# Order of the row minima over PSUM banks, what an exp waits for, and the planned price of a division

## The chip, the cores and the metric

One core of a Trainium2 chip runs one launch. The metric is the device time of the launch in microseconds. Five queues work side by side on the core: PE (TensorE, matrix products), DVE (VectorE), ACT (ScalarE), POOL (GpSimd) and SP (SyncE, which issues the transfers). The inputs are float32 arrays: q, k and v of shape (4, 12, 448, 64), an input matrix 768 x 1024, three rows of convolution weights of 1024, and an output matrix 1024 x 768.

## The reference

Causal attention, and then a gated layer that the program calls FFN. For each batch and head:

```
scores = q @ k.T / sqrt(64), with -1e9 above the diagonal
attn   = exp(scores - rowmax);  attn /= rowsum(attn) + 1e-9
x      = attn @ v                       (heads side by side: 448 x 768)
h      = relu(x @ w_in)                 (448 x 1024)
conv   = conv_w[0]*h[s-1] + conv_w[1]*h[s] + conv_w[2]*h[s+1]
out    = (h * sigmoid(conv)) @ w_out    (448 x 768)
```

## The kernel before

**Attention.** Two heads make a pair, and a batch has 6 pairs, so there are 24 pairs, numbered here from 0. The 448 query rows are cut into 7 blocks of 64 rows; block k of both heads fills the 128 partitions and has 64 (k + 1) keys, so block 6 has 448 columns and block 0 has 64. The scores of a pair lie in four PSUM banks (`SCORES`): bank 0 holds block 6, bank 1 blocks 5 and 1, bank 2 blocks 4 and 0, bank 3 blocks 3 and 2.

For each block, in the order of `RANK`, two steps are written: `least` (line 439, DVE) adds the mask to the scores in place in PSUM and takes the row minimum of the negated scores into one column of `negm`; `expo` (line 445, ACT) reads the scores from PSUM, takes the exponential with that column as bias, writes to SBUF tile `p` and sums the row into one column of `ssum`. Each of the two is followed on its engine by a short instruction that reads the accumulator out. The blocks form two groups, {6, 5, 1} and {4, 3, 2, 0}. When all exps of a group are planned, `r_sum` (line 461, DVE or POOL) adds 1e-9 to the group's sums, `r_inv` (line 464, DVE) inverts them, and `over` divides each block's `p` by its sum, on DVE (line 483) or on ACT (line 487); block 2 takes two instructions, the others one. Then PE transposes `p` in four portions (line 515; the first takes blocks 5 and 6), copies bring them to SBUF (line 523), and PE multiplies with v (lines 543 and 580).

**FFN.** For each batch, PE computes 8 units of x @ w_in (line 626) and 6 of g @ w_out (line 679), each from products of 448 columns; ACT and DVE do the relu, the three taps, tanh and the gate. In the time of the first batch's attention, w_in is also loaded, its words are rearranged on DVE (lines 294 to 320) and split into a rounded part and a rest (lines 253 to 268). w_out follows later.

**What sets the order.** The program writes no order by hand. Class `Plan` holds all steps of the whole kernel, with a nominal cost in ns, the engines that can do it, what it needs and what it makes. It walks a clock of its own: of all steps whose needs are made it takes the one with the smallest start plus a little for its place in the list, gives it to the engine with the earliest weighted end, and writes its instructions. Each engine then runs its instructions strictly in that order. The constants that the prediction uses:

```python
    LAG = {"PE": 200, "DVE": 115, "ACT": 145, "POOL": 40, "SP": 2300}
    OWN = {"PE": 0, "DVE": 115, "ACT": 145, "POOL": 40, "SP": 0}
    EXTRA = {"PE": 100, "POOL": 42}
    WEIGHT = {"DVE": 1.5, "ACT": 1.0, "POOL": 0.5}
                ...
                    due = t + way[1] * self.WEIGHT.get(e, 1.0)
                ...
                late = self.STEP * (s["n"] - head) if s["late"] is None else s["late"]
                rank = (pick[3] + late, s["n"])
```

LAG is the planned delay from the end of a step on one engine to a start on another, OWN that on the same engine, EXTRA is added where PE or POOL has to wait; `early` moves the moment at which a step counts as done. The waits on the chip are not the plan's: the tile framework puts semaphores between instructions, from the order in which they were written and the tiles that they touch.

Batches 2 and 3 (pairs 12 to 23) are **paced** (`paced`, line 417): their scores are one PE step, and each pair starts at a set count of FFN products of the batch before. Batches 0 and 1 are not; their scores are two PE steps, one for each group.

Of the kernel before, what the change touches and what calls it, by code (L numbers as in the profile page):

```python
# [22 lines left out]
class Plan:  # L23
# [25 lines left out]
    def at(self, key):  # L49
        return self.slot[key]  # L50
# [105 lines left out]
def attn_ffn_kernel(ctx: ExitStack, tc: tile.TileContext, qk, v, w_in, conv_w, w_out, out):  # L156
# [8 lines left out]
    nc = tc.nc  # L165
# [9 lines left out]

    SCORES = ((6,), (5, 1), (4, 0), (3, 2))
    SWAPPED = (5, 4, 1, 0)
    RANK = (6, 5, 1, 4, 3, 2, 0)


    BANKS = (((1, 2, 3, 4), 0, 0),), (((5, 6), 0, 0), ((5, 6), 2 * P, 256)), (((6,), None, 0), ((4,), None, 128)), (((3, 4, 5, 6), P, 0),)
# [30 lines left out]
    plan = Plan()  # L212
# [158 lines left out]
    def pair(b, hp):  # L371
# [3 lines left out]
        g = b * NPAIR + hp  # L375
# [27 lines left out]
        def place(k):  # L403
            i = next(i for i, ks in enumerate(SCORES) if k in ks)
            return ("S", g, i), 0 if SCORES[i][0] == k else KEYS[SCORES[i][0]]
# [11 lines left out]
        paced = b > 1 or PACED1 and b == 1  # L417
# [6 lines left out]
        else:  # L424
            for i, blocks in enumerate(((6, 5, 1), (3, 4, 2, 0))):
                plan.add(
                    "PE", 830, lambda blocks=blocks: scores(blocks), makes=[("scores", g, i)], drop=[raw], mode=1,
                    needs=[raw, ("scores", g, 0) if i else ("norm", g - 2)], take=[(("S", "acc") if g < 4 else "S", ("S", g, 2 * i + z)) for z in range(2)],
                )

        groups = RANK[:3], RANK[3:]
        for i, blocks in enumerate(groups):
            for k in blocks:
                n, (s, o), c, (home, h) = KEYS[k], place(k), RANK.index(k), HOME[k]
                p, t = ("p", g, k), ("tile", g, home)

                def least(s=s, o=o, n=n, c=c):
                    t = at(s)[:, o : o + n]
                    nc.vector.tensor_tensor_reduce(  # L439
                        out=t, in0=t, in1=mask[:, S - n :], scale=-0.125, scalar=3.0e38,  # L440
                        op0=ALU.add, op1=ALU.min, accum_out=negm[g % 2][:, c : c + 1],
                    )

                def expo(s=s, o=o, n=n, c=c, t=t, h=h):
                    nc.scalar.activation(  # L445
                        at(t)[:, h : h + n], at(s)[:, o : o + n], AF.Exp, bias=negm[g % 2][:, c : c + 1],
                        scale=-1.0, accum_out=ssum[g % 2][:, c : c + 1],
                    )

                plan.add("DVE", 85 + 1.04 * n, least, needs=[("scores", g, i)], makes=[("least", p)], early=-65)  # L450
                plan.add(
                    "ACT", 237 + 0.83 * n, expo, needs=[("least", p)] + ([("exp", ("p", g, home))] if h else []), early=84,
                    makes=[("exp", g), ("exp", g, i), ("p", g), ("exp", p)], take=[] if h else [(f"p{k}", t)], drop=[s],
                )

        for i, blocks in enumerate(groups):

            cols = slice(3 * i, 3 * i + len(blocks))

            def r_sum(engine, cols=cols):  # L460
                engine.tensor_scalar_add(rcp[g % 2][:, cols], ssum[g % 2][:, cols], 1.0e-9)

            def r_inv(cols=cols):
                nc.vector.reciprocal(out=rcp[g % 2][:, cols], in_=rcp[g % 2][:, cols])  # L464

            plan.add(
                "DVE", 80, lambda f=r_sum: f(nc.vector), other=[("POOL", 250, lambda f=r_sum: f(nc.gpsimd))],
                needs=[("exp", g, i), ("norm", g - 2)], makes=[("r0", g, i)],
            )
            plan.add("DVE", 118, r_inv, needs=[("r0", g, i)], makes=[("r1", g, i)])  # L470
            for k in blocks:
                n, p, c, (home, h) = KEYS[k], ("p", g, k), RANK.index(k), HOME[k]


                def pieces(k=k, n=n, h=h, home=home):
                    t = at(("tile", g, home))
                    if k != 2:
                        return [(t[:, h : h + n], t[:, h : h + n])]
                    return [(t[:, h : h + n - 64],) * 2, (t[:, h - 64 : h], t[:, h + n - 64 : h + n])]

                def over(engine, c=c, pieces=pieces):
                    for to, t in pieces():
                        engine.tensor_scalar_mul(to, t, rcp[g % 2][:, c : c + 1])  # L483

                def over_act(c=c, pieces=pieces):
                    for to, t in pieces():
                        nc.scalar.mul(to, t, rcp[g % 2][:, c : c + 1])  # L487

                plan.add(
                    "DVE", 70 + 0.52 * n + 70 * (k == 2), lambda f=over: f(nc.vector), needs=[("r1", g, i)], makes=[p, ("norm", g)],  # L490
                    port=True, other=[("ACT", 210 + 0.83 * n + 210 * (k == 2), over_act)],
                )

# [2 lines left out]
        for z, y in enumerate(TURNS):  # L496
# [6 lines left out]
            n = P * sum(len(ks) for ks, _, _ in pieces)  # L503

            def transp(pieces=pieces, pt=pt, both=both):
# [13 lines left out]
                makes=[(pt, 1), ("PT", g, y, 1)], take=[("PT", pt)], drop=tiles,  # L519
            )  # L520

            def t_copy(copy, pt=pt, part=part, o=512 * (y % 2), n=n):
# [5 lines left out]
                needs=[(pt, 1)] + ([("pt", g, y + 1, 0)] if y % 2 == 0 else []), makes=[part, ("pt", g, y, 0)],  # L528
# [33 lines left out]
        def x_lo():  # L562
# [4 lines left out]
            needs=[(pv, 1)], makes=[(x, 0)],  # L567
# [138 lines left out]
    with tc.manual_schedule():  # L706
        setup()
        for hp in range(NPAIR):
            pair(0, hp)
            if hp == 2:  # L710
                load_conv(None)
            for i in range(NW):
                if IN_AT[i] == hp:
                    load_w(0, i, None, [("p", hp - 2)])
        for b in range(B):
            if b + 1 < B:
                for hp in range(NPAIR):
                    pair(b + 1, hp)
                    for i in range(NW):
                        if b == 0 and OUT_AT[i] == hp:  # L720
                            load_w(1, i, None, [("p", NPAIR + hp - 3), (("pv", NPAIR - 1), 1)])
            for f in range(NF):
                ffn1(b, f, LATE)
            for m in range(NM):
                ffn2(b, m, LATE)
        plan.run()
# [47 lines left out]
```

## Time and profile before

| | |
|---|---|
| runs | 400.57 us median of 3 (400.37 to 401.91) |
| profiled execution | 401.81 us, of which 400.0 us from the first to the last instruction |
| granted TensorE clock | 1.00 in every stretch |
| PE busy | 376.2 us, 94% of the span |
| DVE, ACT, POOL busy | 261.3, 248.0, 127.9 us |
| row minima (line 439) | 168 on DVE, 68.8 us |
| exps (line 445) | 168 on ACT, 78.7 us, and 36.0 us of accumulator reads |
| divisions | 111 instructions on DVE (31.5 us), 81 on ACT (35.8 us) |

Times are microseconds unless marked ns. An engine's busy time counts its instructions, with those that only wait or branch left out. A matmul's end is modelled, and matmuls overlap: the rows of two that follow each other closely lie over one another.

### The profile page before, as it was taken

The numbers are of one execution on the slowest core, as the hardware profiler recorded it, in microseconds if no ns is written. First come the engines' busy times: TensorE is split into PE (matmuls) and PEld (weight loads), VectorE is DVE, ScalarE is ACT, GpSimd is POOL, SyncE is SP. The second block draws the span as 40 slices with busy tenths as digits, with TensorE's granted clock in tenths as the row PEclk, the third lists the DMA queues.
The fourth block names the chain that finished last, engine by engine and source line by source line (L and its number), as shares of the span: only waits on it lengthen the run. The fifth ranks groups of instructions, "written<-read, shape, count | busy, mean of one in ns | idle before, by whom it ended". The sixth has DMA issues, their size and how long they took to land.

```text
span 400.0 us, 8166 instructions
## 1 busy us (share of the span) xinstructions
PE 376.2 (94%) x2988; PEld 303.5 (76%) x2988; DVE 261.3 (65%) x803; ACT 248.0 (62%) x689; POOL 127.9 (32%) x161
## 2 busy tenths in 40 slices
PE   6888979999999998999989999999989999999996
PEld 3556657876767966787777888888778899999895
DVE  3999999999896674797787052488787100578100
ACT  4899999999997336777676254576675411443111
POOL 2044555455544531226233101035425010334100
PEclk9999999999999999999999999999999999999999
DMA  7984613325257641223113222233010111000111
GB/s 280 404 314 150 225 50 111 100 93 167 72 179 255 191 117 63 76 92 94 40 54 112 75 80 82 70 93 91 5 46 2 48 46 47 2 0 0 48 46 46
DMA packets 15159, 40.65 MB, mean 102 GB/s; under 512 B 1808, under 2 KB 4880, under 8 KB 15120
## 3 DMA queue, kind: packets, MB, share of 16 engines
q1 hardware_dynamic: 15120, 40.14, 30.5%
q8 instruction: 23, 0.38, 0.4%
q14 instruction: 16, 0.13, 0.1%
HBM read 34.63 MB, written 5.51 MB: 100 GB/s over the span
## 4 chain that ended last, share of the span: by engine, by line
PE 41%; DVE 28%; ACT 15%; DMA 6%; issue 6%; POOL 4%; ACTq 0%; POOLq 0%; DVEq 0%
PE bank L679 18%; PE bank L626 11%; DVE bank L439 8%; ACT p L445 7%; PE bank L515 5%; PE bank L580 4%; DVE u L644 4%; DMA wraw<-in_w_in_dram 3%; DMA wraw<-in_w_out_dram 3%; DVE p L483 3%; DVE wraw L320 2%; POOL wol L268 2%; DVE u L314 2%; DVE negm L439 1%; DVE u L596 1%
## 5 line engine op out<-in xcount | busy, mean ns | idle before, releaser
L626 PE MATMUL bank<-parts,wih 128*128 128x448 f32 x384 | 115.9, 377 | 0.0
L679 PE MATMUL bank<-parts,woh 128*128 128x448 f32 x384 | 113.0, 371 | 1.4 <-POOL parts L257 0.6
L445 ACT ACTIVATE p<-bank,negm 128x320 f32<-128x320 f32 (+6 forms) x168 | 78.7, 485 | 19.1 <-DVE negm L439 16.3
L439 DVE CUSTOM_DVE_ANT_0 bank<-bank,mask 128x448 f32<-128x448 f32 (+6 forms) x168 | 68.8, 440 | 15.0 <-PE bank L412 9.6
L679 PEld LDWEIGHTS bank<-parts,woh 128*128 128x128 f32 x384 | 71.4, 188 | 9.2 <-POOL parts L257 1.0
L626 PEld LDWEIGHTS bank<-parts,wih 128*128 128x128 f32 x384 | 70.0, 188 | 6.2 <-issue 1.1
L679 PE MATMUL bank<-parts,wol 128*128 128x448 f32 x192 | 71.5, 372 | 0.9 <-POOL wol L268 0.9
L626 PE MATMUL bank<-parts,wil 128*128 128x448 f32 x192 | 71.9, 375 | 0.0
L515 PE MATMUL bank<-ident,p 128*128 128x128 f32 x336 | 52.3, 281 | 11.3 <-DVE p L483 4.8
L257 POOL TENSOR_SCALAR parts<-u 128x448 fp32r<-128x448 f32 x29 | 17.5, 602 | 140.7 <-DVE u L650 93.5
L644 DVE SCALAR_TENSOR_TENSOR u<-hr,cw,u 128x448 f32<-128x448 f32 x64 | 53.9, 846 | 10.4 <-ACT u L657 9.3
L268 POOL TENSOR_TENSOR parts<-u,parts 128x448 fp32r<-128x448 f32 x44 | 53.0, 1210 | 18.1 <-ACT parts L253 15.9
L515 PEld LDWEIGHTS bank<-ident,p 128*128 128x128 f32 x336 | 37.2, 140 | 26.9 <-ACT p L445 6.8
L523 ACT COPY pt<-bank 128x512 f32<-128x512 f32 (+1 forms) x84 | 43.1, 540 | 10.9 <-PE bank L515 10.3
L412 PE MATMUL bank<-raw 64*64 64x448 f32 (+6 forms) x672 | 45.1, 384 | 3.9 <-ACT p L445 2.4
L412 PEld LDWEIGHTS bank<-raw 64*64 64x64 f32 x672 | 28.6, 133 | 19.5 <-issue 7.8
L690 ACT ACTIVATE u<-bank 128x448 f32<-128x448 f32 x24 | 13.1, 546 | 43.2 <-PE bank L679 43.1
L679 PEld LDWEIGHTS bank<-parts,wol 128*128 128x128 f32 x192 | 36.1, 188 | 4.9 <-POOL wol L268 2.1
L626 PEld LDWEIGHTS bank<-parts,wil 128*128 128x128 f32 x192 | 36.1, 188 | 3.2 <-issue 0.5
L487 ACT ACTIVATE p<-p,rcp 128x64 f32<-128x64 f32 (+5 forms) x81 | 35.8, 491 | 1.1 <-DVE rcp L464 0.9
L445 ACT ACTIVATION_READ_ACCUMULATOR p<-bank,negm 128x1 f32 x168 | 36.0, 214 | 0.0
L483 DVE TENSOR_SCALAR p<-p,rcp 128x128 f32<-128x128 f32 (+5 forms) x111 | 31.5, 340 | 0.8
(47 smaller groups left out, 383.2 us busy)
## 6 DMA issues: line engine op xcount, KB each, us to landing
raw<-in_qk_dram SPq DMA_DIRECT2D x24, 448.0 KB, 4.7
vraw<-in_v_dram SPq DMA_DIRECT2D x24, 448.0 KB, 4.2
wraw<-in_w_in_dram SPq DMA_DIRECT2D x16, 384.0 KB, 7.0
wraw<-in_w_out_dram SPq DMA_DIRECT2D x16, 384.0 KB, 3.6
out_dram<-u SPq DMA_DIRECT2D x24, 224.0 KB, 1.9
wraw<-in_conv_w_dram SPq DMA_DIRECT2D x1, 24.0 KB, 7.7
```

Of the source, the lines that this page charges most:

```text
L257: lambda: nc.gpsimd.tensor_scalar(out=out(), in0=src(), scalar1=1.0, scalar2=1.0, op0=ALU.mult, op1=ALU.mult),
L268: engine.tensor_tensor(out=out(), in0=src(), in1=f32(hi()), op=ALU.subtract)
L412: nc.tensor.matmul(at(s)[half(j ^ (k in SWAPPED)), o : o + KEYS[k]], lhsT=t[:, 1, 64 * k : 64 * k + 64], rhs=t[:, 0, : KEYS[k]], start=Tru ...
L439: nc.vector.tensor_tensor_reduce(out=t, in0=t, in1=mask[:, S - n :], scale=-0.125, scalar=3.0e38, op0=ALU.add, op1=ALU.min, accum_out=negm ...
L445: nc.scalar.activation(at(t)[:, h : h + n], at(s)[:, o : o + n], AF.Exp, bias=negm[g % 2][:, c : c + 1], scale=-1.0, accum_out=ssum[g % 2] ...
L483: engine.tensor_scalar_mul(to, t, rcp[g % 2][:, c : c + 1])
L487: nc.scalar.mul(to, t, rcp[g % 2][:, c : c + 1])
L515: nc.tensor.matmul(to, lhsT=p, rhs=ident, is_transpose=True)
L523: copy(at(part)[:, o : o + n], at(pt)[:, :n])
L626: nc.tensor.matmul(at(ph)[:, :S], lhsT=block(w, NCC * f + cc), rhs=at(x)[:, part], start=q == 0, stop=q == len(prods) - 1)
L644: nc.vector.scalar_tensor_tensor(out=t, in0=src, scalar=w, in1=t, op0=ALU.mult, op1=ALU.add)
L679: nc.tensor.matmul(at(po)[:, :S], lhsT=block(w, NF * m + f), rhs=at(g)[:, part], start=q == 0, stop=q == len(prods) - 1)
```

## The change

The rank of blocks 0 and 2 is swapped, which swaps their columns in `negm`, `ssum` and `rcp` and the order of their divisions. The steps `least` and `expo` are written in a new order of blocks: 6, 5, 4, 1, 3, 0, 2 in a paced pair, and 5, 6, 1, 4, 3, 0, 2 in the others; which group a block belongs to stays. In the plan, an exp needs all minima of its bank (`("least", g, s)`, made by each `least` in bank s) instead of its own alone. The nominal cost of a division on DVE goes from 70 + 0.52 n to 136 + 0.52 n ns, and the addition for block 2 from 70 to 110. PE's scores keep their order.

```diff
-    RANK = (6, 5, 1, 4, 3, 2, 0)
+    RANK = (6, 5, 1, 4, 3, 0, 2)
...
-        for i, blocks in enumerate(groups):
+        for i, blocks in enumerate(((6, 5, 4, 1), (3, 0, 2)) if paced else ((5, 6, 1), (4, 3, 0, 2))):
             for k in blocks:
+                i = RANK.index(k) // 3 and 1
...
-                plan.add("DVE", 85 + 1.04 * n, least, needs=[("scores", g, i)], makes=[("least", p)], early=-65)
+                plan.add("DVE", 85 + 1.04 * n, least, needs=[("scores", g, i)], makes=[("least", g, s), ("least", p)], early=-65)
                 plan.add(
-                    "ACT", 237 + 0.83 * n, expo, needs=[("least", p)] + ([("exp", ("p", g, home))] if h else []), early=84,
+                    "ACT", 237 + 0.83 * n, expo, needs=[("least", g, s)] + ([("exp", ("p", g, home))] if h else []), early=84,
...
-                    "DVE", 70 + 0.52 * n + 70 * (k == 2), lambda f=over: f(nc.vector), needs=[("r1", g, i)], makes=[p, ("norm", g)],
+                    "DVE", 136 + 0.52 * n + 110 * (k == 2), lambda f=over: f(nc.vector), needs=[("r1", g, i)], makes=[p, ("norm", g)],
```

## Rows read from the trace of the kernel before

**Rows 1.** Page, engines' busy time, and the costliest group (busy, mean ns).

```profile
PE 376.2 (94%) x2988; PEld 303.5 (76%) x2988; DVE 261.3 (65%) x803; ACT 248.0 (62%) x689; POOL 127.9 (32%) x161
...
L626 PE MATMUL bank<-parts,wih 128*128 128x448 f32 x384 | 115.9, 377 | 0.0
```

**Rows 2.** Busy time by stage: stretch, length, PE, PEld, DVE, ACT, POOL, clock, DMA.

```profile
4.00:62.00 58.00, 47.75 (x517) 32.36 (x516) 54.24 (x216) 52.31 (x164) 21.26 (x31) 1.00 0.68 238
...
147.00:320.00 173.00, 166.83 (x1475) 136.95 (x1474) 110.32 (x359) 106.11 (x300) 48.71 (x60) 1.00 0.22 68
```

**Rows 3.** Waits of PE alone, 147 to 320 us: total, times, longest.

```profile
PE bank L515 <- DVE p L483: 4.8, 8, 1.1
...
PE bank L515 <- ACT p L487: 0.4, 1, 0.4
PE bank L515 <- ACT u L690: 0.3, 1, 0.3
PE bank L515 <- ACT hr L637: 0.3, 1, 0.3
```

**Rows 4.** Chain of waits, a full run of FFN products: start, length, what.

```profile
177.75 3.26 PE bank L626 x16
```

**Rows 5.** Timeline of PE, pair 16: start, length, line, [idle before <- releaser].

```profile
202.51 0.37 PE L626 MATMUL bank<-parts,wil 128*128 128x448 f32 x1
203.96 0.63 PE L515 MATMUL bank<-ident,p 128*128 128x128 f32 x4 [1.08 <-DVE p L483]
```

**Rows 6.** Timeline of DVE, pair 16.

```profile
199.22 0.62 DVE L439 CUSTOM_DVE_ANT_0 bank<-bank,mask 128x448 f32<-128x448 f32 x1
...
199.76 0.60 DVE L439 CUSTOM_DVE_ANT_0 bank<-bank,mask 128x384 f32<-128x384 f32 x1
200.28 0.14 DVE L439 DVE_READ_ACCUMULATOR2_ANT negm<- 128x1 f32 x1
200.46 0.30 DVE L439 CUSTOM_DVE_ANT_0 bank<-bank,mask 128x128 f32<-128x128 f32 x1
...
200.67 0.53 DVE L439 CUSTOM_DVE_ANT_0 bank<-bank,mask 128x320 f32<-128x320 f32 x1
...
201.12 0.46 DVE L439 CUSTOM_DVE_ANT_0 bank<-bank,mask 128x256 f32<-128x256 f32 x1
...
201.96 0.14 DVE L439 DVE_READ_ACCUMULATOR2_ANT negm<- 128x1 f32 x1
202.47 0.23 DVE L439 CUSTOM_DVE_ANT_0 bank<-bank,mask 128x64 f32<-128x64 f32 x1 [0.37 <-ACT p L445]
...
202.62 0.16 DVE L461 TENSOR_SCALAR rcp<-ssum 128x3 f32<-128x3 f32 x1
...
203.03 0.98 DVE L483 TENSOR_SCALAR p<-p,rcp 128x448 f32<-128x448 f32 x3
203.92 0.16 DVE L461 TENSOR_SCALAR rcp<-ssum 128x4 f32<-128x4 f32 x1
```

**Rows 7.** Timeline of ACT, pair 16.

```profile
199.94 0.64 ACT L445 ACTIVATE p<-bank,negm 128x448 f32<-128x448 f32 x1 [0.58 <-DVE negm L439]
...
200.91 0.58 ACT L445 ACTIVATE p<-bank,negm 128x384 f32<-128x384 f32 x1 [0.24 <-DVE negm L439]
...
201.48 0.36 ACT L445 ACTIVATE p<-bank,negm 128x128 f32<-128x128 f32 x1
...
201.82 0.53 ACT L445 ACTIVATE p<-bank,negm 128x320 f32<-128x320 f32 x1
```

**Rows 8.** Waits of all engines, 147 to 320 us.

```profile
DVE bank L439 <- ACT p L445: 3.6, 10, 0.4
```

**Rows 9.** Timeline of DVE and PE, pair 14.

```profile
170.23 0.62 DVE L439 CUSTOM_DVE_ANT_0 bank<-bank,mask 128x448 f32<-128x448 f32 x1
...
173.62 0.17 DVE L464 RECIPROCAL rcp<-rcp 128x3 f32<-128x3 f32 x1
...
174.76 0.63 PE L515 MATMUL bank<-ident,p 128*128 128x128 f32 x4 [0.28 <-DVE p L483]
```

**Rows 10.** Busy time of line 483 (DVE), then of line 487 (ACT), first stage.

```profile
4.00:62.00 58.00, 7.80 (x27) 1.00 0.68 238
...
4.00:62.00 58.00, 11.27 (x24) 1.00 0.68 238
```

## The prediction

> **What bounds the kernel now.** I read the page first: PE is busy for 376.2 of 400.0 us [rows 1], so a gain has to come from PE's gaps, not from work taken off other engines. Then the stages. From 4 to 62 us (attention of the first batch, conversion of w_in) DVE is busy for 54.24 and ACT for 52.31 of 58 us, PE for 47.75 [rows 2]: there the two vector engines set the pace. From 147 to 320 us, the paced pairs 12 to 23, PE has 166.83 of 173 us and DVE and ACT have over a third of their time free [rows 2]: there only a wait of PE itself costs anything. So I asked for PE's waits in that stretch: nearly all are waits of the first transposes of a pair, for a division, 4.8 us in 8 times and 0.4, 0.3 and 0.3 once each, 5.8 us in 11 of the 12 pairs [rows 3]. The rows understate it: a product's row lasts 0.377 us [rows 1], but in a full run 16 take 3.26 us, 0.204 each [rows 4], so each gap hides another 0.17 behind the modelled end: 5.8 + 11 x 0.17 = **7.7 us** lost.
>
> Why does the division come late? Pair 16, with the first minimum's start (199.22) as zero [rows 6]. DVE starts minimum 5 at the moment at which 6 reads out its accumulator, but minimum 1, in the bank of 5, only after the read-out has ended: the next start is at 200.46, 0.18 after the read-out's start at 200.28. The same happens between 3 and 2. The last minimum, 0, then sits 0.37 us for ACT: it shares bank 2 with block 4, and exp 4, which was written before it, still reads there [rows 6, 7]; ten such waits cost 3.6 us in the paced stage [rows 8]. Behind minimum 0 in DVE's queue stand r_sum and r_inv of group {6, 5, 1}, though its last exp began at 201.48 and took 0.36 [rows 7]. So the divisions begin at 3.81, and the transposes at 4.74, after PE has waited 1.08 us [rows 5, 6]. In pair 14 POOL did r_sum, but r_inv on DVE still stood behind minimum 0, and PE waited 0.28 [rows 9].
>
> The planner knows none of this. By its costs (85 + 1.04 n for a minimum, 237 + 0.83 n for an exp) it sees the minima end at 0.551, 1.035, 1.253, 1.671, 2.022, 2.307 and 2.459, exp 5 start at 1.340 (on the chip 1.69, [rows 7]), exp 1 end at 2.239, r_sum on DVE at 2.459, r_inv at 2.654, divisions 6 and 5 from 2.887 to 3.460, and the transposes ready at 3.675 (LAG 115 and EXTRA 100). The chip is at 4.74: **1.07 late**. With r_sum on POOL the plan has 3.653 against 174.76 - 170.23 = 4.53 on the chip in pair 14 [rows 9]: 0.88 late. PE's queue is strict, so products that could have run first stand behind the transposes.
>
> **The change part by part.**
>
> *Order of minima, paced.* 6, 5, 4, 1, 3, 0, 2 never has two of one bank in a row. The starts of [rows 6] give, from one to the next or to the read-out, 0.54 for 6, 0.52 for 5, 0.21 for 1, 0.45 for 4, 0.15 for 0, and 201.96 - 201.12 - 0.18 = 0.66 for 3 and 2 together, of which I give 3 (256 columns, between the 0.21 of 128 and the 0.45 of 320) 0.38. So the last minimum ends at 2.53 + 0.14 = 2.67, against 3.54 before (202.62 + 0.14). DVE gets 0.87 us back per pair. In this stage that is worth nothing by itself, as DVE has room.
>
> *Exps wait for both minima.* On the chip they do so already: exp 5 began at 200.91, 0.24 after ACT was free, on the read-out of minimum 1 [rows 7]. New on the chip is one thing: exp 4 now follows minimum 0. Queued behind it on ACT are the other exps, the relu and the copies of transposes. Chain: minimum 1 ends at 0.54 + 0.52 + 0.45 + 0.21 + 0.14 = 1.86; exp 5 starts about 0.10 later, at 1.96 (before 1.69). It occupies ACT 0.57 (200.91 to 201.48) to 2.53; minimum 0 was done at 2.39, so exp 4 does not wait. In the plan exp 5 ends at 2.407, exp 4 may start at 2.354 and exp 1 at 1.851; both want 2.407, and the list puts 4 first. So exp 4 (its row of 0.53 less 0.02, as exp 1's 0.36 occupies 0.34) runs to 3.04 and exp 1's sum is out at 3.04 + 0.25 + 0.20 = 3.49, nearly one microsecond later than before. r_sum, at 202.62 or 3.40 before, now comes at 3.57, on a DVE that is free; the divisions start 0.41 later at 3.98, and the transposes 0.93 after that (as before), at **4.91**. The chip's chain becomes 0.17 *longer*.
>
> *What the plan then does.* In the new plan exp 5 starts at 1.671 + 0.180 = 1.851, exp 4 ends at 2.909 and exp 1 at 3.252; r_sum is at 3.313, r_inv at 3.508, and the divisions 6 and 5, now priced 369 and 336, run from 3.741 to 4.446; transposes at **4.661**. The chip's 4.91 is 0.25 late instead of 1.07 or 0.88. PE puts four or five more products before the transposes, and these are needed anyway. Two readings of what is left: every pair stalls 0.25, 12 x 0.25 = 3.0, gain 4.7; or each stall shrinks by the change of misfit (0.63 to 0.82), which leaves 0.4 in the three pairs that now lose 1.08 or about that, and nothing in the rest, gain 6.4. The trace of before has no pair planned this way, so I take the middle, **5.5**; the ends are 0 (DVE fills its new gap with a gate step just before r_sum, and a new wait takes the place) and 7.7. Next late would be the portions that need group {4, 3, 0, 2}: its last sum is out at about 4.7, in time for DVE, which divides the first group until about 4.9; no such stall shows now, and I charge none.
>
> *First stage.* In pairs 0 to 7 two minima of one bank follow each other directly 11 times out of 16 (the pattern of rows 6), 11 x 0.17 = 1.9, and pair 0 has one wait of 0.37 like that of rows 6: 2.3 us of DVE. DVE is busy 94% there, but ACT 90% [rows 2], so ACT is late next; between 0 and 2.3 I take half, 1.1. Against it: with 5 before 6, the first exp of a pair starts one minimum (0.52) later. ACT's other work covers that except in pair 0, where exp 5 follows exp 6 directly: exp 6 would end 6 and 5 together plus 0.63 after the first start, 1.06 + 0.20 + 0.63 = 1.89, where exp 5 started at about 1.7 before: 0.2. Uncovered everywhere it would be 8 x 0.2 = 1.6. Net **0.9**, ends -1.6 and 2.3.
>
> *Dearer division.* In the plan DVE's weighted price for n = 448 goes from 454 to 553 and for block 2 from 360 to 519; ACT's are 582 and 579. DVE still wins from an equal start, so a division moves only where ACT is free 0.1 to 0.16 us sooner than before. A division took 7.80 / 27 = 0.29 us on DVE and 11.27 / 24 = 0.47 on ACT [rows 10]; three in a row on DVE are spaced (203.92 - 203.03) / 3 = 0.30 [rows 6], and the new price averages 0.30 for these three, the old 0.24. So the plan gets truer. I expect about 4 of 27 to move in the first stage: ACT +1.9 of 5.7 free, DVE -1.2: cost nothing. Bounds: nothing, and all 27 (rival C).
> The Trainium skill, page "ScalarE: Activation LUTs", section "Rules for kernel authors", tells authors to put plain multiplications on VectorE and not on ScalarE; the 0.29 against 0.47 agrees, and by that rule this edit alone is a loss, the way of rival C.
>
> Sum: 5.5 + 0.9 = 6.4 us. The profiled execution (401.81, 400.0 of it span) would go to 395.4; it lies 1.24 above the median of the runs, so the median goes from 400.57 to **394.2**.
>
> **The rivals.**
> A, the forecast: 394.2, with a range of its own from 7.7 + 2.3 = 10.0 gained (390.6) to a remaining stall of twice 0.25 and no gain in the first stage, 7.7 - 6.0 = 1.7 (398.9).
> B, a new wait takes the old one's place: r_sum or r_inv, planned at 3.3 to 3.6, leaves DVE a gap of about 0.85 that a tap or gate step fills, and PE waits on the division as long as now. For it: the chip's chain is 0.17 longer. Against: the planner books that step too. Only the first stage gains: 399.7.
> C, slower: divisions flood ACT in the first stage. Each moved one costs ACT 0.47; the 5.7 us free are gone at 12, all 27 make 12.7, 7.0 too many. DVE's savings are then worth nothing there; against the lower reading of the paced gain, 4.7, the end is +2.3: 402.9. It decides from (5.7 + 4.7) / 0.47 = 22 moved. Against it: DVE keeps the lower price at an equal start.
> D, the edit does not do what it says: the 0.18 between neighbours is not the bank's but the small tile's, and minimum 0 still waits for ACT: 400.5. Against: minimum 4 after 1 starts with no such gap, at 200.67 [rows 6].
>
> **How the numbers follow.** A 0.70, B 0.15, C 0.10, D 0.05. About 0.5%, 2 us, is what a measurement of this kernel can tell from no change. Faster than 398.57: 0.67 of A and 0.02 of B, 0.69. Same: 0.03 of A, 0.12 of B, 0.04 of D, 0.19. Slower: C, and 0.02 of B and D, 0.12. The range leaves out C and the outer ends: 390.5 to 401.0.
>
> **What would show it.** In the profile after: the waits of PE's line 515 on divisions from 147 to 320 us fall from 5.8 to under 3 us; no wait of line 439 on ACT in paced pairs; seven minima of a paced pair in about 2.7 us instead of 3.54; exp order 6, 5, 4, 1; the first transposes about 4.9 after the first minimum, with more products ahead of them. It is wrong if these waits keep their size (B), if line 487 grows from 24 to over 36 instructions before 62 us (C), or if what the paced stage gains is lost in the tail or by new waits in the stage of w_out.

## The result and the profile after

The changed kernel takes 397.79 us in the median of 9 runs (394.85 to 399.11), against 401.15 (400.37 to 403.19, 9 runs) before: a ratio of 0.9901, with a 95% interval of 0.9871 to 0.993. Six later runs gave 0.9906 (0.9886 to 0.9925). The forecast was 394.2 and a ratio of 0.984. The profiled execution took 399.11 us, with a span of 397.3; it is the slowest of the nine. The six later runs have a profile too (397.81 us, span 396.0), called the second profile here.

The same stages as in [rows 2], of the changed kernel (columns as there, the clock being the last but two):

```profile
4.00:62.00 58.00, 48.76 (x484) 33.10 (x484) 50.45 (x199) 50.99 (x156) 18.71 (x28) 0.94 0.64 226
62.00:106.00 44.00, 43.53 (x354) 33.47 (x351) 42.12 (x118) 43.13 (x126) 22.30 (x25) 1.00 0.38 122
106.00:147.00 41.00, 39.24 (x271) 31.72 (x269) 34.66 (x91) 29.09 (x81) 18.37 (x20) 0.96 0.58 181
147.00:320.00 173.00, 171.41 (x1520) 141.98 (x1521) 114.33 (x362) 106.77 (x305) 52.02 (x62) 1.00 0.21 68
```

Two things are to be seen. In the paced stage PE is busy for 171.41 us where it was 166.83. And two stages have a granted clock below 1.00, which no stage of the profile before has. In the stage of 0.96 the fall is this short stretch:

```profile
119.60:123.00 3.40, 3.40 (x13) 2.56 (x12) 3.40 (x10) 2.79 (x7) 0.43 (x1) 0.50 0.44 165
```

The waits of PE between 147 and 320 us in the changed kernel, which answer to [rows 3] (total, times, longest):

```profile
PE bank L680 <- POOL wol L268: 0.4, 1, 0.4
PE bank L516 <- ACT p L488: 0.4, 2, 0.2
PE bank L680 <- ACT woh L253: 0.3, 1, 0.3
PE bank L516 <- DVE rcp L462: 0.2, 1, 0.2
PE bank L516 <- DVE p L484: 0.2, 1, 0.2
```

The transposes (now line 516) wait 0.8 us in all, where it was 5.8. The ten waits of a minimum for ACT [rows 8] have no row any more in DVE's list.

From the first minimum of pair 12 to the end of the last product with v, the trace before has 147.00 to 319.19 us, and 514 FFN products start between them; the trace after has 152.06 to 316.82 with 510. That is 172.2 against 164.8, and four products of 0.204 have to be added to the latter: **6.6 us won in the paced stage**. Not all of it need be the change's. One run below (`e12_before_fill`) has the plan of the kernel before and its waits for divisions, and wins 1.2 us on the same measure. The two profiles differ near pair 12, where PE waited for the split words of w_out before, and in that run not at all. Waits of PE before, 140 to 160 us:

```profile
PE bank L679 <- POOL wol L268: 0.9, 2, 0.5
PE bank L679 <- ACT woh L253: 0.3, 1, 0.3
```

So by this comparison the change won between 5.4 and 6.6 us there. But pair 12 starts 5.1 us later, with four products more done before it, 0.8 us worth: **4.2 us lost before it**. The second profile has 6.6 won again, but 2.7 lost. In the first, 2.9 of the 4.2 are there when pair 6 starts (53.98 instead of 51.11, after 24 products in both); the rest comes later, with the second fall of the clock shown above. At 21 us it was 4.8 us late (the first products with v begin at 20.84 instead of 16.05), so a part of that is made up by pair 6.

How the start went wrong is told by some short pieces of timeline. The first minimum, after and before, and before each the first scores of PE:

```profile
5.15 2.62 PE L412 MATMUL bank<-raw 64*64 64x448 f32 x28
7.29 0.57 DVE L440 CUSTOM_DVE_ANT_0 bank<-bank,mask 128x384 f32<-128x384 f32 x1 [6.35 <-PE bank L412]
```

```profile
4.57 1.75 PE L412 MATMUL bank<-raw 64*64 64x448 f32 x28
5.71 0.63 DVE L439 CUSTOM_DVE_ANT_0 bank<-bank,mask 128x448 f32<-128x448 f32 x1 [4.77 <-PE bank L412]
```

The first minimum starts 1.58 us later, and at least 0.9 of that is not the edit's: the same 28 products took 2.62 us instead of 1.75, and in the second profile of the same kernel they took 1.75 again and the first minimum started at 6.38. What follows is in both profiles of the changed kernel. PE of the changed kernel (start, length, shape of the first, number, [idle before <- releaser]):

```profile
5.15 2.62 PE L412 MATMUL bank<-raw 64*64 64x448 f32 x28
8.05 1.09 PE L412 MATMUL bank<-raw 64*64 64x448 f32 x12 [0.28 <-DMA raw<-in_qk_dram]
11.56 0.97 PE L412 MATMUL bank<-raw 64*64 64x256 f32 x16 [2.42 <-ACT p L446]
13.09 0.63 PE L516 MATMUL bank<-ident,p 128*128 128x128 f32 x4 [0.55 <-DVE p L484]
14.88 1.12 PE L516 MATMUL bank<-ident,p 128*128 128x128 f32 x4 [1.16 <-ACT p L488]
15.92 1.99 PE L412 MATMUL bank<-raw 64*64 64x448 f32 x12
```

ACT of the changed kernel, and then of the kernel before:

```profile
8.58 1.28 ACT L446 ACT_TABLE_LOAD   x1 [8.58 <-DVE negm L440]
9.88 0.63 ACT L446 ACTIVATE p<-bank,negm 128x448 f32<-128x448 f32 x1
```

```profile
0.72 1.28 ACT L445 ACT_TABLE_LOAD   x1 [0.72 <-PEq L758]
6.44 0.63 ACT L445 ACTIVATE p<-bank,negm 128x448 f32<-128x448 f32 x1 [4.44 <-DVE negm L439]
```

Before, ACT loads its activation table (an instruction of its own ahead of the first exp) at 0.72, with nothing else to do. After, the load stands behind the wait for the first minima, on the path: the first exp comes 9.88 - 7.29 = 2.59 us after the first minimum's start instead of 6.44 - 5.71 = 0.73 (second profile: 2.58). In the instruction streams, the first exp waits for one semaphore before (DVE's), and for two after (DVE's and PE's), and the first of the two waits is on the table load. With block 5's minimum ahead of 6's, the wait on DVE alone seems no longer to cover PE's scores; the six-first run below has one semaphore again, and the load at 0.72.

PE waits 2.42 us for these exps to release a bank, and soon 0.55 and 1.16 more. Then the granted clock falls from the upper level (2.4 GHz) to the lower (1.2 GHz). Stretches of the changed kernel (length, busy PE, PEld, DVE, ACT, POOL, clock, DMA share, GB/s):

```profile
0.00:13.80 13.80, 9.27 (x72) 4.87 (x72) 5.85 (x31) 5.21 (x17) 2.45 (x12) 1.00 0.87 311
13.80:20.60 6.80, 5.72 (x38) 3.67 (x38) 4.62 (x25) 5.36 (x21) 0.00 (x0) 0.50 1.03 402
```

The same stretch before:

```profile
13.80:20.60 6.80, 6.21 (x73) 4.03 (x71) 6.61 (x33) 6.66 (x25) 0.59 (x2) 1.00 1.03 402
```

PE ran 38 matrix instructions there instead of 73. Twelve products of the scores took 1.99 us at 15.92, against 1.09 at 8.05 at the upper level. The Trainium skill, page "TensorE: Matmul & The Clock Gate", section "HAM oscillation — how this bites in real kernels", describes that waits between groups of PE's work let the clock fall back; here the fall follows the three waits above, and the row has 0.50. That waits of this size are not all that decides is shown below (paced pairs alone).

The mean granted clock of each run tells how regular this is. Medians in us (and number of runs) by that clock, over all runs of this study that list it:

| kernel | up to 0.989 | 0.990 to 0.992 | 0.994 to 0.996 | 0.998 to 1.000 | mean clock |
|---|---|---|---|---|---|
| before | | 403.57 (7) | 401.94 (33) | 400.35 (23) | 0.996 |
| after | 397.94 (12) | 396.70 (2) | | 394.85 (1) | 0.988 |

At a like clock the change would be worth 403.57 - 396.70 = 6.9 us or 400.35 - 394.85 = 5.5 us, but this rests on two runs and one of the changed kernel. The kernel as it stands keeps 3.4 to 3.8 us, and 12 of its 15 runs have a mean clock of 0.989 or less; both of its profiles, at 0.986 and 0.987, have the falls near 14 and near 120 us.

### The profile page after: what moved, and what is told of

Its sections match the earlier page's. It is cut to its first block, busy times and chain, and to the rows that moved or that the text cites. A ratio compares the mean times of both kernels' runs of the same rounds, so it can differ in the third digit from the quotient of the medians.

```text
span 397.3 us, 8173 instructions
## 1 busy us (share of the span) xinstructions
PE 379.2 (95%) x2988; PEld 308.1 (78%) x2988; DVE 264.2 (66%) x800; ACT 247.8 (62%) x697; POOL 126.8 (32%) x156
## 4 chain that ended last, share of the span: by engine, by line
PE 59%; DVE 19%; ACT 12%; issue 3%; DMA 3%; POOL 2%; ACTq 0%; DVEq 0%; POOLq 0%
PE bank L680 22%; PE bank L627 19%; PE bank L516 7%; ACT p L446 5%; PE bank L412 5%; PE bank L581 5%; DVE bank L440 4%; DVE u L314 3%; DVE wraw L320 3%; DMA wraw<-in_w_out_dram 2%; ACT p L488 2%; DVE u L645 2%; ACT pt L524 1%; ACT u L294 1%; DVE u L651 1%
## 5 line engine op out<-in xcount | busy, mean ns | idle before, releaser
L680 PE MATMUL bank<-parts,woh 128*128 128x448 f32 x384 | 115.3, 375 | 1.2 <-ACT parts L253 0.6
L627 PEld LDWEIGHTS bank<-parts,wih 128*128 128x128 f32 x384 | 71.5, 188 | 6.9 <-issue 0.7
L440 DVE CUSTOM_DVE_ANT_0 bank<-bank,mask 128x384 f32<-128x384 f32 (+6 forms) x168 | 66.3, 450 | 13.9 <-PE bank L412 13.9
L268 POOL TENSOR_TENSOR parts<-u,parts 128x448 fp32r<-128x448 f32 x44 | 54.3, 1238 | 27.5 <-ACT parts L253 25.0
L645 DVE SCALAR_TENSOR_TENSOR u<-hr,cw,u 128x448 f32<-128x448 f32 x64 | 55.0, 860 | 4.9 <-ACT u L658 3.7
L516 PEld LDWEIGHTS bank<-ident,p 128*128 128x128 f32 x336 | 38.5, 144 | 19.9 <-ACT p L488 7.1
L412 PE MATMUL bank<-raw 64*64 64x448 f32 (+6 forms) x672 | 47.9, 399 | 4.3 <-ACT p L446 4.0
L412 PEld LDWEIGHTS bank<-raw 64*64 64x64 f32 x672 | 30.1, 138 | 21.0 <-issue 9.5
L488 ACT ACTIVATE p<-p,rcp 128x64 f32<-128x64 f32 (+5 forms) x93 | 41.7, 503 | 2.4 <-DVE rcp L465 2.1
L648 ACT ACTIVATE u<-u 128x448 f32<-128x448 f32 x32 | 18.7, 585 | 16.4 <-DVE u L645 16.3
```

The costliest lines, as they stand in the source:

```text
L268: engine.tensor_tensor(out=out(), in0=src(), in1=f32(hi()), op=ALU.subtract)
L412: nc.tensor.matmul(at(s)[half(j ^ (k in SWAPPED)), o : o + KEYS[k]], lhsT=t[:, 1, 64 * k : 64 * k + 64], rhs=t[:, 0, : KEYS[k]], start=Tru ...
L440: nc.vector.tensor_tensor_reduce(out=t, in0=t, in1=mask[:, S - n :], scale=-0.125, scalar=3.0e38, op0=ALU.add, op1=ALU.min, accum_out=negm ...
L516: nc.tensor.matmul(to, lhsT=p, rhs=ident, is_transpose=True)
L627: nc.tensor.matmul(at(ph)[:, :S], lhsT=block(w, NCC * f + cc), rhs=at(x)[:, part], start=q == 0, stop=q == len(prods) - 1)
L645: nc.vector.scalar_tensor_tensor(out=t, in0=src, scalar=w, in1=t, op0=ALU.mult, op1=ALU.add)
```

## The experiments

Two theories were weighed first. S (start): the paced gain is whole, and what is missing went in the first 20 us. P (price): the dearer division floods ACT in the first stage. Ratios are to the kernel before on the same chip, with 95% intervals.

**The table load off the path.** One tiny exp at the start of ACT's queue; the rest in the same order.

```diff
+    spark = sb.tile([P, 24], F32, name="spark")
...
     def setup():
+        nc.gpsimd.memset(spark, 0.0)
+        nc.scalar.activation(spark, spark, AF.Exp)
```

> The changed kernel with one tiny exp on a small tile of zeros added at the start of ACT's queue, so that the activation table is loaded there; all else in the same order. Theory S (start): the change gives about 6.8 us in the paced stage and loses about 4.8 us in the first 20 us; of that loss 1.28 us is the table load, which in the changed kernel stands behind ACT's wait for the first minima. Then the first exp starts about 1.3 us sooner (8.6 instead of 9.88), PE's second scores and all that follows too, and the time falls by 1.3 to 3 us from that of the change: ratio to before 0.983 to 0.987. Theory P (price): the loss comes from the dearer division, which sends more divisions to ACT in the first stage; then the start doesn't decide and the ratio stays at 0.990.

0.9881 (0.985 to 0.9912), 397.25 us. In its profile the first exp starts 1.31 us after the first minimum's start, where it was 2.59: the load is gone from the path. But the clock still falls, from 13.9 to 17.4 us (0.52 in the row below), and the time gain over the change, 0.2%, is within the intervals. Expected were 0.983 to 0.987: a miss. Taking the load alone off the path gains nothing that can be told from noise.

```profile
13.90:17.40 3.50, 3.50 (x21) 2.04 (x20) 2.01 (x12) 2.33 (x9) 0.00 (x0) 0.52 1.03 405
```

**Minimum 6 first again in batches 0 and 1.**

```diff
-        for i, blocks in enumerate(((6, 5, 4, 1), (3, 0, 2)) if paced else ((5, 6, 1), (4, 3, 0, 2))):
+        for i, blocks in enumerate(((6, 5, 4, 1), (3, 0, 2)) if paced else ((6, 5, 1), (4, 3, 0, 2))):
```

> The changed kernel, but in batches 0 and 1 the minima of the first group in the order 6, 5, 1 instead of 5, 6, 1 (1 is next to 5 again there). Theory S: the first exp needs only the first minimum, and the table load has no wait before it, so the first exp is at about 6.4 as before; ratio 0.980 to 0.985. Theory P: 0.990, as the price is kept. A theory that the bank neighbours matter in the first stage expects about 12 x 0.17 = 2 us more: 0.995.

0.9891 (0.9856 to 0.9927). The first exp is 0.73 after the first minimum, and the mean clock is back at 0.997, as theory S has it; yet the time is no better: a miss (0.980 to 0.985). In its profile the transposes of the paced stage wait 2.3 us (1.6 and 0.7) instead of 0.8. Measured as above, it loses 0.5 us before pair 12, so the loss at the start is gone, as S has it; but from pair 12 on it wins 4.4 instead of 6.6. The other order in the first batches also gave another plan for the later ones, and the two about cancel.

**Order and wait in the paced pairs alone.**

```diff
-        for i, blocks in enumerate(((6, 5, 4, 1), (3, 0, 2)) if paced else ((5, 6, 1), (4, 3, 0, 2))):
+        for i, blocks in enumerate(((6, 5, 4, 1), (3, 0, 2)) if paced else ((6, 5, 1), (4, 3, 2, 0))):
...
-                    "ACT", 237 + 0.83 * n, expo, needs=[("least", g, s)] + ([("exp", ("p", g, home))] if h else []), early=84,
+                    "ACT", 237 + 0.83 * n, expo, needs=[("least", g, s) if paced else ("least", p)] + ([("exp", ("p", g, home))] if h else []), early=84,
```

> Order of minima and wait of the exps changed in the paced pairs alone (batches 2 and 3); in batches 0 and 1 minima in the old order 6, 5, 1, 4, 3, 2, 0 and each exp planned after its own minimum. New price of the division everywhere. Theory S: the whole gain of the paced stage, none of the loss at the start: 0.982 to 0.986. Theory P: 0.990 or above.

0.9852 (0.9813 to 0.9891): theory S's figure, and against P, whose price is kept, though the interval overlaps that of the change. PE's line 516 waits 0.4 us in the paced stage. The mean clock is still 0.989, so the order of the first minima was not the only thing that let it fall. Nor does the length of PE's waits alone decide it: up to 15 us PE waits 0.30, 0.78, 1.29 and 0.42 us here and 0.27, 0.81, 1.38 and 0.29 in the run before, but the clock from 13.8 to 20.6 us is 0.81 here and 1.00 there.

**The price alone**, on the kernel before.

```diff
-                    "DVE", 70 + 0.52 * n + 70 * (k == 2), lambda f=over: f(nc.vector), needs=[("r1", g, i)], makes=[p, ("norm", g)],
+                    "DVE", 136 + 0.52 * n + 110 * (k == 2), lambda f=over: f(nc.vector), needs=[("r1", g, i)], makes=[p, ("norm", g)],
```

> The kernel before with the new price of the division alone (136 + 0.52 n, 110 more for block 2). Theory S: little, 0.997 to 1.003, with the stalls of the first transposes in the paced stage still at 4 to 6 us by PE's waits. Theory P: slower, 1.004 to 1.012, with the loss between 5 and 62 us. If the price is what makes the plan true, the paced stalls shrink by a fifth and the ratio is 0.995 or less.

0.9957 (0.9933 to 0.9982), 12 runs, with the same clock as before (0.997). It gains, so theory P (1.004 to 1.012) falls, and the gain is more than S allowed (0.997 to 1.003). In its profile PE waits 2.7 us in the paced stage for divisions (2.5 and 0.2) instead of 5.2; the minima still wait for ACT, 3.7 us in 10.

**The change with the old price.**

```diff
-                    "DVE", 136 + 0.52 * n + 110 * (k == 2), lambda f=over: f(nc.vector), needs=[("r1", g, i)], makes=[p, ("norm", g)],
+                    "DVE", 70 + 0.52 * n + 70 * (k == 2), lambda f=over: f(nc.vector), needs=[("r1", g, i)], makes=[p, ("norm", g)],
```

> The changed kernel with the old price of the division (70 + 0.52 n, 70 more for block 2). The price alone took the first transposes' stalls in the paced stage from 7.7 to 6.2 us in the gaps between PE's instructions and made the kernel 0.4% faster. If price and order add up, this lies at 0.993 to 0.996 with paced stalls of 3 to 4.5 us; if the order with its wait does all that is to be done, it stays at 0.990 with stalls under 3; if the price costs time in the first stage, it is faster, 0.985.

0.9933 (0.9905 to 0.9962). PE waits 2.2 us for divisions, five times. At mean clocks of 0.990 to 0.992 its 7 runs have a median of 398.37, 1.7 above the two of the change. So the price and the rest (order and wait) add up, roughly: 0.9957 x 0.9933 = 0.9890.

**The wait in the plan alone**: the old order and price, each exp planned behind both minima of its bank.

```diff
-                plan.add("DVE", 85 + 1.04 * n, least, needs=[("scores", g, i)], makes=[("least", p)], early=-65)
+                plan.add("DVE", 85 + 1.04 * n, least, needs=[("scores", g, i)], makes=[("least", g, s), ("least", p)], early=-65)
                 plan.add(
-                    "ACT", 237 + 0.83 * n, expo, needs=[("least", p)] + ([("exp", ("p", g, home))] if h else []), early=84,
+                    "ACT", 237 + 0.83 * n, expo, needs=[("least", g, s)] + ([("exp", ("p", g, home))] if h else []), early=84,
```

> The kernel before with the exps planned behind both minima of their bank, in the old order of minima and at the old price. Theory of the truer plan: the plan learns of the wait that the chip has anyway, so the first transposes are planned later and stall less, 3 to 5 us instead of 7.7: ratio 0.992 to 0.997. Rival, that the order itself (no two of a bank in a row, minimum 0 never behind exp 4) makes the gain: 0.998 to 1.002 with stalls as before.

0.9949 (0.992 to 0.9977). PE's waits for divisions fall from 5.2 to 1.2 us, with the old order. The chip did the wait of exp 5 for minimum 1 before as well [rows 7]; that of exp 4 for minimum 0 is new, and the minima's waits for ACT are gone from DVE's list here too. So it is not shown apart whether the plan's knowledge pays or the end of these waits; but the price alone keeps them (3.7 us in 10) and gains all the same.

**The order alone**, in the paced pairs, on the kernel before: the new rank and order of minima, each exp planned after its own minimum, the old price.

```diff
-    RANK = (6, 5, 1, 4, 3, 2, 0)
+    RANK = (6, 5, 1, 4, 3, 0, 2)
-        for i, blocks in enumerate(groups):
+        for i, blocks in enumerate(((6, 5, 4, 1), (3, 0, 2)) if paced else ((6, 5, 1), (4, 3, 2, 0))):
             for k in blocks:
+                i = RANK.index(k) // 3 and 1
```

> The kernel before with the new order of minima and the new rank in the paced pairs alone; exps planned after their own minimum, old price. Rival of the order: most of the paced gain, 0.985 to 0.992, stalls under 4 us. Theory of the truer plan: the minima of a pair take 2.8 us instead of 3.5, but exps start later than planned (exp 5 waits for minimum 1, which is now behind 4), so the stalls stay at 6 us or more: 0.996 to 1.003.

1.0048 (1.0026 to 1.0069): *slower*. The plan still takes exp 4 before minimum 0, and the waits of minima for ACT are 4.6 us in 12, more than before. PE's waits (total, times, longest), 147 to 320 us:

```profile
PE bank L516 <- DVE p L484: 3.2, 9, 0.5
PE bank L516 <- ACT p L488: 0.4, 1, 0.4
```

Neither expectation (0.985 to 0.992, and 0.996 to 1.003) foresaw that. Measured as above, the paced stage gains 0.6 us, and 1.6 are lost before pair 12. It has also the lower clock, 0.991 in the mean; at 0.990 to 0.992 its 10 runs have 403.10, and the kernel before has 403.57. So the loss lies ahead of the paced stage and goes with the lower clock; that the clock is its cause is not shown. The headline of the change, neighbours in different banks, is not what makes it faster.

**Does PE's idle time near 10 us make the clock fall, and does that cost time?** 14 products of zeros, as in the warm-up, behind the second pair's first scores, in the changed kernel.

```diff
+        def fill(n):
+            for _ in range(n):
+                nc.tensor.matmul(bank[4][:, :384], lhsT=bank_zeros[:, :P], rhs=bank_zeros[:, :384], start=True, stop=True)
...
+            if g == 1 and 6 in blocks:
+                fill(14)
```

> The changed kernel with 14 products of zeros (128 x 384, the same as the 12 at the start) on PE after the second pair's first scores, where PE has nothing to do from about 9.1 to 11.6 us; they write a bank that is overwritten later. Theory C (clock): PE's idle time near 10 us makes the chip grant the lower of its two clock levels from about 13.8 us on, for 3 to 7 us, and this costs a part of the gain. Then the granted clock has no stretch at the lower level near 14 us, its mean rises from 0.987 to 0.993 or more, and the time falls to 395 to 396.5. Rival: the lower clock costs nothing there, as ACT and DVE set the pace; then the time stays at 397 to 398 with the higher mean clock. Second rival: the products are in the way, 398 or more.

0.9854 (0.9816 to 0.9892), 395.14 us, the foreseen 395 to 396.5. Its profile has PE go on from 8.62 to 11.0 with the zeros, and no lower clock near 14 us:

```profile
0.00:13.80 13.80, 10.46 (x88) 5.83 (x89) 6.92 (x37) 6.51 (x22) 2.46 (x12) 1.00 0.87 324
13.80:20.60 6.80, 6.76 (x83) 4.31 (x82) 6.38 (x35) 6.80 (x25) 0.22 (x1) 1.00 1.03 401
20.60:62.00 41.40, 36.98 (x369) 26.39 (x369) 39.45 (x144) 39.90 (x124) 20.03 (x27) 0.96 0.53 179
```

Useless work of 2.4 us goes with a faster kernel, although the table load was still on the path. The interval still touches those of the change; the next runs are the surer comparison.

**Four together on one chip**: the change again, the paced version with the zeros, the change with zeros and the early exp, and the kernel before with 8 products of zeros behind the second pair's last scores. The first has no edit; the second and third join the edits shown above; the fourth has `fill` as above, and

```diff
+            if g == 1 and 0 in blocks:
+                fill(8)
```

> The changed kernel once more, on the chip of the three kernels beside it, as their yardstick. All theories: 0.988 to 0.993, mean granted clock mostly 0.985 to 0.991.

> Order and wait changed in the paced pairs alone, new price everywhere, and the 14 products of zeros after the second pair's first scores. Theory S and C together: the paced gain, no table load on the path and no stretch at the lower clock near 13 us: 0.977 to 0.983 (392 to 394 us), clock 0.995 or more. If the order 5, 6, 1 of the first batches was worth something by itself, it is no better than the changed kernel with the products, 0.985.

> The changed kernel with both: the tiny exp at the start of ACT's queue and the 14 products of zeros. Theory S: the table load is worth about 1.3 us on top of the products alone, 0.980 to 0.983. Rival: the products already hide what the table load costs, since PE is kept at the higher clock; then 0.985 as with the products alone.

> The kernel before with 8 products of zeros after the second pair's scores, where PE waits 1.3 us for ACT. Theory C for the changed kernel alone: here the clock is 0.996 in the mean already, so there is at most 1 us to win: 0.997 to 1.002. Rival, that the products help whatever the kernel: 0.993 to 0.995, and then the gain of the products in the changed kernel is no answer to where the gain of the change went.

| kernel | us | ratio | interval | mean clock |
|---|---|---|---|---|
| the change again | 398.23 | 0.9906 | 0.9886 to 0.9925 | 0.987 |
| paced alone, with zeros | 396.78 | 0.9866 | 0.9846 to 0.9886 | 0.990 |
| change, zeros, early exp | **394.42** | 0.9808 | 0.9786 to 0.983 | 0.998 |
| before, with zeros | 401.03 | 0.9982 | 0.9964 to 1.0 | 0.999 |

The change with zeros and early exp is the fastest kernel of the study: 3.8 us under the change, and the intervals lie apart. So most of what the change lost before pair 12 can be had back. The zeros do the larger part: with the early exp alone it was 0.9881 (0.985 to 0.9912), an interval that lies apart from 0.9786 to 0.983, though the chips differ. What the load adds to the zeros is not settled: 0.9808 and 0.9854 stand on different chips with touching intervals. Nor is all of it won at 14 us. The plan is the same as that of the change, and from the first minimum of pair 11 to that of pair 12 this kernel takes 33.09 us, the change 34.70 and 34.54 in its two profiles: the fall near 120 us is gone too, and why is open.

Before, the zeros bring 0.2% (0 to 0.4), though they lift the clock from 0.996 to 0.999; they are no general cure. The paced version missed its 0.977 to 0.983, and here the zeros brought nothing: it had 0.9852 without them. The first fall is mended, but the fall in the stage of w_out is there with them and without (116 to 124 us: 0.57 in the third row of these windows, 0.61 without; columns as above), and the 1.1 us that it is ahead at pair 11 are gone at pair 12 (150.10 and 150.08 us). So a fall of the clock that is taken away does not always give time back:

```profile
9.00:16.00 7.00, 6.46 (x63) 4.05 (x65) 6.53 (x36) 6.79 (x26) 0.71 (x3) 1.00 1.04 408
100.00:116.00 16.00, 12.65 (x105) 9.52 (x103) 15.90 (x50) 15.26 (x44) 7.73 (x11) 1.00 0.44 139
116.00:124.00 8.00, 6.78 (x43) 4.52 (x42) 5.28 (x11) 5.22 (x18) 2.97 (x4) 0.57 0.45 129
```

**All profiles by the same measure.** The start of the first minimum; what is won from pair 12's first minimum to the last product with v; what is lost before pair 12, both against the profile before, with 0.204 us for each FFN product done sooner or later. They are single executions: the last row says how far two of one plan can differ, and so do the two of the change.

| kernel | first minimum at | won from pair 12 on | lost before it |
|---|---|---|---|
| before | 5.71 | | |
| order alone | 6.79 | 0.6 | 1.6 |
| price alone | 6.29 | 3.3 | 0.5 |
| wait in the plan alone | 6.50 | 3.8 | 3.2 |
| order and wait, old price | 6.38 | 4.3 | 0.5 |
| the change, both profiles | 7.29, 6.38 | 6.6, 6.6 | 4.2, 2.7 |
| six first | 6.86 | 4.4 | 0.5 |
| paced alone | 6.75 | 6.2 | 1.2 |
| paced alone, zeros | 7.08 | 6.2 | 1.3 |
| change, early exp | 7.35 | 6.2 | 2.5 |
| change, zeros | 5.99 | 6.6 | -0.8 |
| change, zeros, early exp | 6.28 | 6.2 | -0.5 |
| before, zeros | 6.46 | 1.2 | -0.3 |

## Why the prediction was right, and where it was not

**The paced stage: right.** The forecast was 5.5 us, between 4.7 and 6.4 by two readings; measured are 5.4 to 6.6. The waits fell to 0.8 us (foreseen: under 3). Pair 16 of the changed kernel, on DVE, against [rows 6]:

```profile
199.97 0.62 DVE L440 CUSTOM_DVE_ANT_0 bank<-bank,mask 128x448 f32<-128x448 f32 x1
...
202.28 0.40 DVE L440 CUSTOM_DVE_ANT_0 bank<-bank,mask 128x192 f32<-128x192 f32 x1
202.60 0.14 DVE L440 DVE_READ_ACCUMULATOR2_ANT negm<- 128x1 f32 x1
202.82 0.45 DVE L643 TENSOR_SCALAR u<-hr,cw 128x448 f32<-128x448 f32 x1
203.31 1.41 DVE L645 SCALAR_TENSOR_TENSOR u<-hr,cw,u 128x448 f32<-128x448 f32 x2
204.85 0.18 DVE L465 RECIPROCAL rcp<-rcp 128x3 f32<-128x3 f32 x1
205.06 0.65 DVE L484 TENSOR_SCALAR p<-p,rcp 128x448 f32<-128x448 f32 x2
```

The seven minima take 202.74 - 199.97 = 2.77 us (worked out: 2.67; before: 3.54). On ACT and PE, against [rows 5, 7]:

```profile
202.17 0.55 ACT L638 ACTIVATE hr<-bank 128x448 f32<-128x448 f32 x1 [0.76 <-PE bank L627]
202.61 0.57 ACT L446 ACTIVATE p<-bank,negm 128x384 f32<-128x384 f32 x1
...
203.17 0.53 ACT L446 ACTIVATE p<-bank,negm 128x320 f32<-128x320 f32 x1
...
203.67 0.38 ACT L446 ACTIVATE p<-bank,negm 128x128 f32<-128x128 f32 x1
```

```profile
205.62 0.37 PE L680 MATMUL bank<-parts,woh 128*128 128x448 f32 x1
205.84 0.33 PE L516 MATMUL bank<-ident,p 128*128 128x128 f32 x1
```

Exp 4 runs before exp 1, as the tie in the list said. The divisions and transposes came even later than worked out (5.09 and 5.87 after the first minimum, not 3.98 and 4.91): the planner used the wait of exp 5 for a relu, and the gap on DVE for three taps. That is what rival B foresaw, but the plan booked these steps too, so PE went on with products until 205.84 and the transposes found their data: the objection to B was right. The chain that was worked out is 1 us too short, and the gain did not hang on it. The chain of a pair became longer by 1.1 us, and the kernel faster.

**What of the change did it.** The prediction put the gain in the truer plan, and the runs agree: in the paced stage the wait known to the plan wins 3.8 us alone, the price 3.3, the order 0.6, less than two profiles of one plan differ. Price and wait are both corrections of the planner's picture. That the price edit alone would be a loss did not come out: hardly a division moved (24 to 25 on ACT in the first stage), and the kernel gained (0.9957).

**The first stage: wrong.** "Net 0.9" won, with a loss of 1.6 as its worst end, should have been a loss of 2.7 to 4.2 before pair 12. The failed step is "with 5 before 6, the first exp of a pair starts one minimum (0.52) later", with its price of 0.2. The 0.52 was seen; what was not is that the first exp's second semaphore puts the table load behind its wait (1.28 us: 8.58 to 9.86), so that the first exp came 2.59 us after the first minimum's start instead of 0.73, and that PE then ran at a granted clock of 0.50 from 13.8 to 20.6 us. The zeros and the early exp gave 3.8 us back; how much of that is the load's, the clock's at 14 us and the clock's near 120 us stays open. The larger loss, 4.2, has at least 0.9 us in it that is chance of the execution: the first minimum of that profile came late by itself. The Trainium skill, page "ScalarE: Activation LUTs", section "What ACT_TABLE_LOAD costs", gives 1.28 us for the load, as in the rows here; of a further drain that it adds, the rows show nothing, as the exp starts 0.02 after the load's end. Whether DVE won anything there could not be told apart from these losses: with the zeros, pair 12 starts 0.5 to 0.8 us sooner than before, near the 0.9 forecast, but the starts of one kernel's executions differ by as much.

**The number.** 397.79 us lies in the stated range, and that says little, as the range of 390.5 to 401.0 holds the time before as well. What bears the mechanism out is that the waits fell as foreseen.

**Rivals.** A came out, at its unfavourable side, which it had put down to a stall that remains in the paced stage; it was the first stage that lost. C did not: line 487's 24 divisions in the first stage became 25 in line 488, and 23 stayed on DVE. D is out: the waits on ACT are gone, and each minimum of pair 16 starts at the moment at which the one before reads out.

## What to carry to other kernels

Where a planner orders strict queues, a wait that the chip does and the plan doesn't know costs twice: once itself, and once by what is put behind it. It can pay to tell the plan of it, even if the chain gets longer, where the engine that bounds the kernel has other work to do first. After a reordering, look at the first microseconds: which semaphores the first activation waits for, and whether PE goes idle there. And take a second profile of the same kernel before a difference of 1 to 2 us is put down to an edit.

## What the runs showed of the hardware that was not expected

Fourteen products of zeros in an idle stretch of 2.4 us of PE kept the granted clock at 1.00 from 13.8 to 20.6 us where it had been 0.50. With the early exp they took the kernel from 398.23 to 394.42 us; in the paced version they lifted the clock of that stretch from 0.81 to 1.00 as well, and the time stayed (0.9852 and 0.9866). And executions of one program differ in mean clock and in time: from 0.991 to 1.000, the medians of the kernel before go from 403.57 to 400.35 us, which is about as much as the whole change brings. The two go together; that the clock is the whole of it is not shown.
